# Order of weight loads, small stores and last steps in a one-core attention-and-MLP backward kernel

## Chip, core and metric

The kernel runs on one core of one Trainium2 chip. The metric is the device time of one execution in microseconds. Before the change three runs gave 430.39, 437.87 and 425.78 us, median 430.39.

## What is computed

The reference is one decode step of a gated mixture of a multi-head attention block over a K/V cache and a small MLP, and its gradients with respect to all inputs but the MLP's own x.

```python
x: [1, 1, 640]; k_cache, v_cache: [1, 32, 4096, 128]; wq: [640, 4096]; wo: [4096, 640]
w1: [640, 1728]; b1: [1728]; w2: [1728, 640]; gate_w: [640]; all bf16

g = sigmoid(sum(x * gate_w))
q = (x @ wq) as 32 heads of 128;  p = softmax(q . K * 128**-0.5);  a = (p . V) @ wo
h = B_x @ w1 + b1;  b = (h * tanh(softplus(h))) @ w2
out = g * a + (1 - g) * b
```

Outputs are `out` and the gradients of x, K, V, wq, wo, w1, b1, w2 and gate_w. dK and dV have the size of the caches: 67 MB are read for K and V and 67 MB written for their gradients. In the code out_2 is dK, out_3 dV, out_4 dwq, out_5 dwo, out_6 dw1, out_7 db1 and out_8 dw2.

## The kernel before

**Pairs and slots.** The 32 heads are worked through as 16 pairs (index i), each pair's K or V being one tile [128, 8192] of 2 MB. Eight such buffers (`kv0` to `kv7`) are in use. Every pair has 16 slots (function `slot`, line 687). In slots 0 to 7 TensorE transposes an eighth of V of pair i (line 342), ScalarE copies it out (`tch`, line 345), and two or three slots later products with the columns of dO make dP (line 352); slots 8 to 15 do the same with K of pair i+1 and q, for the scores S of the next pair. Between them lies the chain of the pair: maximum (slots 2 and 4), exponentials (5), sum (7), p (8), o (column sums on TensorE, 7 and 8, line 401), D (10), dS (11), and dq (13 and 14). dV is made over V in place by four VectorE outer products (slots 9, 10, 12, 13, line 433) and stored at slot 13; dK of pair i-1 is made over K (slots 15 of the pair before, 0, 1, 3) and stored at slot 3.

**Groups.** Four pairs form a group g of eight heads, with one slice of wq (`wqb`, [128, 5, 1024]) and one of wo (`wob`, [128, 8, 640]), both double-buffered by g % 2. Before a group starts, the kernel needs its query rows and columns (`q_half` twice, line 259, then `q_cols`, 268) and its dO rows and columns (`do_sum` eight times on VectorE, 271; `do_rows`, 275; `do_cols`, 283; `do_plain`, 286). After its pairs it makes the share of a (`o_rows`, 298; `a_cols`, 310), overwrites wo by dwo on ScalarE (`dwo_row`, eight times, 322) and stores it (`st_dwo`, 325), and for each of five row chunks takes dx's sum over wq on VectorE (`dx_sum`, 452) and overwrites wq by dwq on ScalarE (`dwq_row`, 457), then stores that (`st_dwq`, 460). Only then can the weights of group g+2 be loaded there (`ld_wo`, 152; `ld_wq`, 149).

**The order of the work** is written out by hand: `at(i, s, f, ...)` (line 593) hangs a step behind the body of slot s of pair i, and every engine runs its instructions in the order in which they are issued. `cols(i, s, g, c0, c1)` (line 596) hangs five `dx_sum` on slots s to s+4 and five `dwq_row` on s+1 to s+5, for the columns c0 to c1 of the group.

**Queues.** Loads are issued on SyncE (SP). `pump` (line 168) issues the next K or V load as soon as a buffer has been given back, right behind the step that stores it; on the chip SP then waits until that store has landed. Loads of weights wait in the same way for the store of the weights that they replace. Stores of dK, dV and the weights are issued on GpSimd (POOL) as long as loads are left, afterwards on SP. ScalarE (ACT) issues the db1 stores, the last part of dwo and the three final vectors.

**Scratch shared between steps.** All of `spread`, `q_half`, `pair_cols`, `do_rows`, `o_rows` and `a_cols` use one PSUM tile (`misc`), and `spread` and `pair_cols` share the SBUF tile `dup`.

**Start and end.** At the start SP issues the first loads, POOL the loads of x, gate_w, dy and b1 (lines 173 to 176) and then the identity `idf` (179 to 184). From x come the gate and, from it and dy, da and db; `spread` (234) broadcasts them over partitions. At the end (lines 795 to 843) pair 15 is written out without its slots 12 to 15: dV, dK in four quarters, dq, and the last share of a, wq, wo and the three vectors.

Of the kernel before, what the change touches and what calls it, by code (L numbers as in the profile page):

```python
# [17 lines left out]
def kernel(  # L18
# [83 lines left out]
    def C(shape, dt, name):  # L102
        return const.tile(shape, dt, name=name, tag=name)
# [64 lines left out]
    def pump():  # L168
        while loads and (free_q or not loads[0][0]):
            loads.popleft()[1]()  # L170

    pump()
    for t, src in ((xc[:], x_v), (gwc[:], vec_cols(gate_w)), (dyc[:], dy_v),
# [5 lines left out]
    idf = C([P, P], F32, "idf")  # L179
    nc.gpsimd.memset(idf[:], 0.0)  # L180
    nc.gpsimd.affine_select(
        out=idf[:], in_=idf[:], compare_op=ALU.not_equal, fill=1.0,
        base=0, pattern=[[-1, P]], channel_multiplier=1,
    )
# [382 lines left out]
    def mlp_dh():  # L567
        nc.vector.tensor_tensor(dh_b[:], dact[:], dm[:], ALU.mult)
        nc.scalar.dma_start(out_7[0:FM].rearrange("(p k) -> p k", k=FK), dh_b[:, 0:FK])
        nc.scalar.dma_start(out_7[FM:F].rearrange("(p o) -> p o", o=1), dh_b[0:FR, FK:FN])  # L570

    def mlp_dhrow(h):
        spread(dh_b[:, 0:FK], FK, 64 * h, 64 * h + 64, dh_bc[:, 64 * h * FK:(64 * h + 64) * FK])
        if h:
            ps = misc([P, FR], BF16, "dh_ps")
            nc.tensor.transpose(ps[:], dh_b[0:FR, FK:FN].to_broadcast([FR, P]), idb[0:FR, 0:FR])
            nc.scalar.copy(dh_bc[:, FM:F], ps[:])

# [14 lines left out]
    def at(i, s, f, *a):  # L593
        side.setdefault((i, s), []).append(lambda: f(*a))
# [6 lines left out]
    KC = 6 * Dh  # L601
    for g in range(1, NG):
        i = 4 * g - 1
        at(i, 4, q_half, g, 0)
        at(i, 6, q_half, g, 1)
        at(i, 8, q_cols, g)
        for k in range(8):
            if g == 1:
                at(i, (3, 4, 4, 5, 6, 7, 8, 8)[k], do_sum, g, k)
            else:  # L610
                at(i - 1, (3, 4, 5, 6, 7, 8, 14, 14)[k], do_sum, g, k)
        at(i, 10, do_rows, g)
        at(i, 12, do_cols, g)
        at(i, 14, do_plain, g)
    for g in range(NG):
        i = 4 * g + 3
        last = g == NG - 1
        at(i - last, 10, o_rows, g, 0, P - 32 * last)
        at(i - last, 11, a_cols, g)
        for k in range(8):  # L620
            at(i - last, 12 + k // 2, dwo_row, g, k, 0, P - 32 * last)
        if g == 0:
            cols(4, 4, 0, 0, GC)
        else:
            cols(i, 4, g, 0, KC)
            if not last:
                cols(i + 1, 4, g, KC, GC)
        if last:
            at(i, 0, st_dwo, g, nc.sync, 0, P - 32)
            at(i, 10, st_dwq, g, 0, KC, nc.sync)  # L630
        else:
            at(i + 1, 0, st_dwo, g, nc.gpsimd)
            at(i + 1, 10, st_dwq, g, 0, GC, nc.gpsimd)
            if g + 2 < NG:
                at(i + 1, 8, ld_wo, g + 2)
                at(i + 1, 15, ld_wq, g + 2)
# [134 lines left out]
    spread(da_c[:], RC, 0, P, da_bc[:])  # L771
    q_half(0, 0)
    q_half(0, 1)
    q_cols(0)
# [24 lines left out]
    for s in range(9, 12):  # L799
        slot(i, s)  # L800
    for t in (2, 3):
        outer(vbuf[i], st[i]["p"], Dr[g % 2][:, q, :], t)
    nc.sync.dma_start(dVv[i], bufs[vbuf[i]][:, 0:KVW])
    fb = free_q.popleft()
# [4 lines left out]
    col_sum(i, "dq", kbuf[i], ds_m[i % 2], 0, J)  # L809
    dq_row(i)  # L810
    o_rows(g, 32 * q, P)
    a_cols(g)
# [4 lines left out]
    for k in range(8):  # L817
        dwo_row(g, k, 32 * q, P)
    st_dwo(g, nc.scalar, 32 * q, P)
# [54 lines left out]
```

## Time and profile before

| | |
|---|---|
| median of three runs | 430.39 us (425.78 to 437.87) |
| profiled execution | 430.21 us, its span 428.4 us |
| mean granted TensorE clock | 0.872 |
| busy: TensorE matmul, VectorE, ScalarE | 315.7, 278.2, 269.2 us |
| DMA | 164.89 MB, mean 385 GB/s |
| SP's wait for dK and dV stores | 303.4 us in 26 waits |
| ScalarE's wait for transposes (line 342) | 58.5 us in 65 waits |

The span runs from the first to the last instruction of the profiled execution; the profile's DMA rows cut it in 40 slices of 10.71 us. A digit is the busy share in tenths, and 9 is 90% or more. The row of GB/s tells what the sixteen DMA engines moved. In a timeline row the bracket gives the engine's idle time ahead of the instruction and what ended it; POOL and SP rows ending in `DMA_DIRECT2D` are issues, not transfers. A row of a table of stretches has the stretch, its length, then for PE, PEld (weight load), DVE, ACT and POOL the busy time and the number of instructions, then the granted TensorE clock, the DMA engines' busy share and GB/s.

Pair i begins its first slot (by the `tch` copies of line 345) at these times: 34.3, 53.9, 74.6, 98.4, 137.0, 158.7, 183.3, 199.6, 241.4, 256.1, 273.6, 299.7, 335.3, 350.0, 365.7 and 390.1 us.

### The profile page before, as it was taken

How to read it: one execution, taken by the hardware profiler on the slowest of the kernel's cores; microseconds unless marked ns; L12 is line 12 of the kernel's file. 1: busy time of each engine (PE TensorE's matmuls, PEld its weight loads, DVE VectorE, ACT ScalarE, POOL GpSimd, SP SyncE). 2: the span in 40 equal slices, each digit the busy share in tenths (PEclk: the TensorE clock that was granted, in tenths of full speed). 3: DMA queues.
4: the chain of work that ended last, by engine and by line, in shares of the span. 5: the costliest groups of instructions: out<-in, count | busy, mean ns of one | idle time of the engine just before them, and what ended most of it. 6: DMA issues, size and time to landing. Idle time of an engine off the chain costs nothing. (4 is left out here: it accounts for less than half of the span.)

```text
span 428.4 us, 13140 instructions
## 1 busy us (share of the span) xinstructions
PE 315.7 (74%) x5679; PEld 287.2 (67%) x5682; DVE 278.2 (65%) x612; ACT 269.2 (63%) x542; POOL 22.3 (5%) x45
## 2 busy tenths in 40 slices
PE   3569798886685896788667898829669899889320
PEld 3159698884684786677456897829558799878320
DVE  3271659997635894999435686737754696577950
ACT  3245455579657887575463987525485987759452
POOL 3000000001000010000000010000000000000000
PEclk9998899998957987999875999978896999979755
DMA  8999999999999999999999999999999997999781
GB/s 271 438 424 414 417 417 372 379 405 359 182 430 429 426 418 393 425 429 419 430 427 431 420 419 408 424 422 425 424 434 404 410 362 258 384 427 369 317 324 31
DMA packets 17465, 164.89 MB, mean 385 GB/s; under 512 B 2288, under 2 KB 3632, under 8 KB 7680
## 3 DMA queue, kind: packets, MB, share of 16 engines
q1 hardware_dynamic: 11328, 101.09, 58.6%
q0 software_dynamic: 5376, 62.63, 36.3%
q8 instruction: 44, 0.72, 0.6%
q10 hardware_dynamic: 704, 0.34, 0.5%
q14 instruction: 13, 0.11, 0.1%
HBM read 82.03 MB, written 82.03 MB: 383 GB/s over the span
## 5 line engine op out<-in xcount | busy, mean ns | idle before, releaser
L345 ACT COPY tch<-tr 128x512 f32<-128x512 f32 x256 | 145.8, 587 | 64.8 <-PE tr L342 58.5
L342 PE MATMUL tr<-idf,kv 128*128 128x128 f32 x1024 | 177.1, 301 | 8.5 <-DMA kv<-in_A_k_cache_dram 8.5
L342 PEld LDWEIGHTS tr<-idf,kv 128*128 128x128 f32 x1024 | 122.7, 154 | 15.7 <-issue 13.7
L352 PEld LDWEIGHTS <-tch 128*128 128x128 bf16 x2048 | 91.7, 100 | 43.4 <-ACT tch L345 35.5
L433 DVE TENSOR_TENSOR kv<-ds_dup,Qr 128x2048 bf16<-128x2048 bf16 x64 | 76.6, 1220 | 2.9 <-ACT tch L345 1.5
L433 DVE TENSOR_TENSOR kv<-p_dup,Dr 128x2048 bf16<-128x2048 bf16 x64 | 76.9, 1219 | 0.7 <-ACT p_dup L392 0.3
L401 PEld LDWEIGHTS <-kv 128*128 128x128 bf16 x2048 | 63.5, 100 | 7.1 <-DVE ds_m L423 3.9
L352 PE MATMUL dP<-dR,tch 128*128 128x48 bf16 x1024 | 48.5, 187 | 21.5 <-ACT tch L345 21.1
L352 PE MATMUL S<-qR,tch 128*128 128x48 bf16 x1024 | 49.8, 189 | 9.3 <-ACT tch L345 6.6
L401 PE MATMUL dq<-ds_m,kv 128*128 128x48 bf16 x1024 | 34.6, 191 | 6.4 <-DVE ds_m L423 6.2
L401 PE MATMUL o<-e_m,kv 128*128 128x48 bf16 x1024 | 32.6, 186 | 0.0
L272 DVE SCALAR_TENSOR_TENSOR junk<-wo,da_bc 128x640 bf16<-128x640 bf16 x32 | 26.3, 821 | 8.2 <-DMA wo<-in_A_wo_dram 7.5
L323 ACT ACTIVATE wo<-da_bc,o8f 128x640 bf16<-128x640 bf16 (+2 forms) x40 | 30.6, 822 | 0.1
L458 ACT ACTIVATE wq<-dqrow,xf 128x768 bf16<-128x768 bf16 (+2 forms) x35 | 26.9, 781 | 3.5 <-DVE wq L454 3.0
L680 POOL DMA_DIRECT2D out_dram<-kv x24 | 12.9, 538 | 264.9 <-DVE kv L433 226.9
L454 DVE SCALAR_TENSOR_TENSOR wq<-wq,dqrow 128x768 bf16<-128x768 bf16 (+2 forms) x35 | 25.4, 761 | 0.2
L407 DVE TENSOR_TENSOR o<-o,rz 128x2 f32<-128x2 f32 x16 | 2.5, 158 | 31.4 <-PE o L401 31.4
L262 PE MATMUL q_ps<-wq,xc 128*128 128x512 bf16 x37 | 13.8, 505 | 8.4 <-DMA wq<-in_A_wq_dram 6.9
L379 ACT ACTIVATE e_m<-S,negM 64x64 bf16<-64x64 f32 x32 | 10.5, 328 | 12.4 <-DVE negM L374 11.9
L386 DVE RECIPROCAL rz<-z 128x2 f32<-128x2 f32 x16 | 2.7, 170 | 23.3 <-PE z L384 23.2
L392 ACT ACTIVATE p_dup<-e_m,rz 64x128 bf16<-64x128 bf16 x32 | 12.7, 397 | 5.5 <-DVE rz L386 4.9
L374 DVE TENSOR_REDUCE negM<-mt 64x1 f32<-64x64 f32 x32 | 7.1, 222 | 12.6 <-PE mt L371 11.8
(162 smaller groups left out, 252.7 us busy)
## 6 DMA issues: line engine op xcount, KB each, us to landing
out_dram<-kv POOLq DMA_DIRECT2D x24, 2048.0 KB, 17.2
kv<-in_A_v_cache_dram SPq DMA_DIRECT2D x16, 2048.0 KB, 19.4
kv<-in_A_k_cache_dram SPq DMA_DIRECT2D x15, 2048.0 KB, 18.8
out_dram<-kv SPq DMA_DIRECT2D x7, 2048.0 KB, 14.9
wq<-in_A_wq_dram SPq DMA_DIRECT2D x4, 1280.0 KB, 34.3
wo<-in_A_wo_dram SPq DMA_DIRECT2D x4, 1280.0 KB, 22.6
out_dram<-wo POOLq DMA_DIRECT2D x3, 1280.0 KB, 12.1
out_dram<-wq POOLq DMA_DIRECT2D x3, 1280.0 KB, 14.5
```

Of the source, the lines that this page charges most:

```text
L262: nc.tensor.matmul(ps[:].rearrange("p a h d -> p (a h d)"), lhsT=xc[:, rc:rc + 1].to_broadcast([P, P]), rhs=wqb[g % 2][:, rc, a * 512:(a + ...
L272: nc.vector.scalar_tensor_tensor(junk[:], in0=wob[g % 2][:, k, :], scalar=1.0, in1=da_bc[:], op0=ALU.mult, op1=ALU.mult, accum_out=do8[g % ...
L323: nc.scalar.mul(wob[g % 2][p0:p1, k, :], da_bc[p0:p1, :], o8f[p0:p1, k:k + 1])
L342: nc.tensor.transpose(tp[:, t, :], src[:, 4 * c + t, :], idf[:])
L345: nc.scalar.copy(dst[:].rearrange("p a b e -> p (a b e)").bitcast(F32), tp[:].rearrange("p a b -> p (a b)"))
L352: nc.tensor.matmul(ps[:, 4 * B:4 * B + W].rearrange("p (a b) -> p a b", b=4), lhsT=src[:, t, :, e], rhs=col[:, e, :, :].rearrange("p a b - ...
L392: nc.scalar.activation(p[HS[hh]], e_m[i % 2][HS[hh], :, hh].unsqueeze(2).to_broadcast([64, J, 2]), ACT.Copy, scale=st[i]["rz"][HS[hh], hh: ...
L401: nc.tensor.matmul(st[i][key][:].rearrange("p (a b) -> p a b", b=2), lhsT=src[:, j, :], rhs=rhs[:, j, :].unsqueeze(1).to_broadcast([P, W / ...
L433: nc.vector.tensor_tensor(kview(b)[:, j0:j0 + n, :].rearrange("p j (a b) -> p j a b", b=2), col[:, j0:j0 + n, :].unsqueeze(2).to_broadcast ...
L454: nc.vector.scalar_tensor_tensor(w, in0=w, scalar=1.0, in1=dqrow[g % 2][:, c0:c1], op0=ALU.mult, op1=ALU.mult, accum_out=dq_acc[:, rc, par ...
L458: nc.scalar.mul(wqb[g % 2][:, rc, c0:c1], dqrow[g % 2][:, c0:c1], xf[:, rc:rc + 1])
L680: eng.dma_start(dst, bufs[b][:, 0:J * Dh])
```

## The change

- The identity is built on POOL ahead of the five small loads.
- db1 was stored from `dh_b` by two DMAs (13 values per partition, and one value in each of 64 partitions). It is now stored as one row of 1728 values from `dh_bc`, which holds db1's values in every partition, behind the last copy into it.
- In the start, the two `q_half` of group 0 go ahead of da's `spread`.
- For groups 1 to 3, `q_half` moves from slots 4 and 6 to 6 and 8 and `q_cols` from 8 to 9; for groups 2 and 3, `do_sum` moves from the pair before (slots 3 to 8, and two at 14) to two at slot 14 of that pair and six at slots 3 to 8 of the group's last pair before it starts.
- `cols` of groups 1 and 2 is cut in two halves of 512 columns, the first one pair earlier (pair 4g+2, slots 4 on), the second at pair 4g+4 from slot 2 on; before it was 768 columns at pair 4g+3 and 256 at 4g+4 from slot 4 on. Group 0 and the last group keep theirs.
- `st_dwq` of group 1 and 2 moves from slot 10 to 8. `ld_wo` moves from slot 8 to slot 1, right behind `st_dwo` in slot 0, and `ld_wq` from 15 to 11 (group 0) or 9 (group 1).
- At the end, the dq sum, `o_rows` and `a_cols` go ahead of the last two dV outer products, and `dq_row`, the dwo rows and their store ahead of the dK outer products.

```diff
+    (idf: memset and affine_select moved here)
     pump()
     for t, src in ((xc[:], x_v), (gwc[:], vec_cols(gate_w)), (dyc[:], dy_v), ...
         nc.gpsimd.dma_start(t, src)
-    (idf stood here)
...
     def mlp_dh():
         nc.vector.tensor_tensor(dh_b[:], dact[:], dm[:], ALU.mult)
-        nc.scalar.dma_start(out_7[0:FM].rearrange("(p k) -> p k", k=FK), dh_b[:, 0:FK])
-        nc.scalar.dma_start(out_7[FM:F].rearrange("(p o) -> p o", o=1), dh_b[0:FR, FK:FN])
...
             nc.scalar.copy(dh_bc[:, FM:F], ps[:])
+            nc.scalar.dma_start(out_7.rearrange("(o f) -> o f", o=1), dh_bc[0:1, :])
...
     for g in range(1, NG):
         i = 4 * g - 1
-        at(i, 4, q_half, g, 0)
-        at(i, 6, q_half, g, 1)
-        at(i, 8, q_cols, g)
+        at(i, 6, q_half, g, 0)
+        at(i, 8, q_half, g, 1)
+        at(i, 9, q_cols, g)
         for k in range(8):
             if g == 1:
                 at(i, (3, 4, 4, 5, 6, 7, 8, 8)[k], do_sum, g, k)
+            elif k < 2:
+                at(i - 1, 14, do_sum, g, k)
             else:
-                at(i - 1, (3, 4, 5, 6, 7, 8, 14, 14)[k], do_sum, g, k)
+                at(i, 1 + k, do_sum, g, k)
...
-            cols(i, 4, g, 0, KC)
-            if not last:
-                cols(i + 1, 4, g, KC, GC)
+            cols(i - 1, 4, g, 0, GC // 2)
+            cols(i + 1, 2, g, GC // 2, GC)
-            at(i + 1, 10, st_dwq, g, 0, GC, nc.gpsimd)
+        at(i + 1, 10 if g == 0 else 8, st_dwq, g, 0, GC, nc.gpsimd)
             if g + 2 < NG:
-                at(i + 1, 8, ld_wo, g + 2)
-                at(i + 1, 15, ld_wq, g + 2)
+            at(i + 1, 1, ld_wo, g + 2)
+            at(i + 1, 11 if g == 0 else 9, ld_wq, g + 2)
...
-    spread(da_c[:], RC, 0, P, da_bc[:])
     q_half(0, 0)
     q_half(0, 1)
+    spread(da_c[:], RC, 0, P, da_bc[:])
     q_cols(0)
...
+    col_sum(i, "dq", kbuf[i], ds_m[i % 2], 0, J)
+    o_rows(g, 32 * q, P)
+    a_cols(g)
     for t in (2, 3):
         outer(vbuf[i], st[i]["p"], Dr[g % 2][:, q, :], t)
     nc.sync.dma_start(dVv[i], bufs[vbuf[i]][:, 0:KVW])
+    dq_row(i)
+    for k in range(8):
+        dwo_row(g, k, 32 * q, P)
+    st_dwo(g, nc.scalar, 32 * q, P)
     fb = free_q.popleft()
     for t in range(4):
         outer(fb, st[i]["ds"], Qr[g % 2][:, q, :], t)
         h = slice(t * KVW // 4, (t + 1) * KVW // 4)
         nc.sync.dma_start(dKv[i][:, h], bufs[fb][:, h])
-    col_sum(i, "dq", kbuf[i], ds_m[i % 2], 0, J)
-    dq_row(i)
-    o_rows(g, 32 * q, P)
-    a_cols(g)
     for rc in range(RC):
         dx_sum(g, g, KC, GC, rc)
         dwq_row(g, KC, GC, rc)
     st_dwq(g, KC, GC, nc.sync)
-    for k in range(8):
-        dwo_row(g, k, 32 * q, P)
-    st_dwo(g, nc.scalar, 32 * q, P)
```

More of the change, by code (lines that the diff above doesn't have):

```diff
@@ L170, in pump @@
             loads.popleft()[1]()
-    pump()
-    for t, src in ((xc[:], x_v), (gwc[:], vec_cols(gate_w)), (dyc[:], dy_v),
-                   (b1c[:, 0:FK], B_b1[0:FM].rearrange("(p k) -> p k", k=FK)),
-                   (b1c[0:FR, FK:FN], B_b1[FM:F].rearrange("(p o) -> p o", o=1))):
-        nc.gpsimd.dma_start(t, src)
     idf = C([P, P], F32, "idf")
@@ L184 @@
     )
+    pump()
+    for t, src in ((xc[:], x_v), (gwc[:], vec_cols(gate_w)), (dyc[:], dy_v),
+                   (b1c[:, 0:FK], B_b1[0:FM].rearrange("(p k) -> p k", k=FK)),
+                   (b1c[0:FR, FK:FN], B_b1[FM:F].rearrange("(p o) -> p o", o=1))):
+        nc.gpsimd.dma_start(t, src)
     ones_b = C([P, 1], BF16, "ones_b")
@@ L599, in cols @@
             at(i, s + 1 + rc, dwq_row, g, c0, c1, rc)
-    KC = 6 * Dh
     for g in range(1, NG):
         i = 4 * g - 1
-        at(i, 4, q_half, g, 0)
-        at(i, 6, q_half, g, 1)
-        at(i, 8, q_cols, g)
+        at(i, 6, q_half, g, 0)
+        at(i, 8, q_half, g, 1)
+        at(i, 9, q_cols, g)
         for k in range(8):
@@ L614 @@
         at(i, 14, do_plain, g)
-    for g in range(NG):
+    for g in range(NG - 1):
         i = 4 * g + 3
-        last = g == NG - 1
-        at(i - last, 10, o_rows, g, 0, P - 32 * last)
-        at(i - last, 11, a_cols, g)
+        at(i, 10, o_rows, g)
+        at(i, 11, a_cols, g)
         for k in range(8):
-            at(i - last, 12 + k // 2, dwo_row, g, k, 0, P - 32 * last)
+            at(i, 12 + k // 2, dwo_row, g, k)
+        at(i + 1, 0, st_dwo, g, nc.gpsimd)
         if g == 0:
@@ L624 @@
         else:
-            cols(i, 4, g, 0, KC)
-            if not last:
-                cols(i + 1, 4, g, KC, GC)
[L628 to L632, printed above, removed]
-            at(i + 1, 10, st_dwq, g, 0, GC, nc.gpsimd)
-            if g + 2 < NG:
-                at(i + 1, 8, ld_wo, g + 2)
-                at(i + 1, 15, ld_wq, g + 2)
+            cols(i - 1, 4, g, 0, GC // 2)
+            cols(i + 1, 2, g, GC // 2, GC)
+        at(i + 1, 10 if g == 0 else 8, st_dwq, g, 0, GC, nc.gpsimd)
+        if g + 2 < NG:
+            at(i + 1, 1, ld_wo, g + 2)
+            at(i + 1, 11 if g == 0 else 9, ld_wq, g + 2)
+    KC = 6 * Dh
+    g, i = NG - 1, NP - 1
+    at(i - 1, 10, o_rows, g, 0, P - 32)
+    at(i - 1, 11, a_cols, g)
+    for k in range(8):
+        at(i - 1, 12 + k // 2, dwo_row, g, k, 0, P - 32)
+    at(i, 0, st_dwo, g, nc.sync, 0, P - 32)
+    cols(i, 4, g, 0, KC)
+    at(i, 10, st_dwq, g, 0, KC, nc.sync)
     at(0, 12, lambda: spread(db_c[:], RC, 0, P, db_bc[:]))
@@ L803 @@
     nc.sync.dma_start(dVv[i], bufs[vbuf[i]][:, 0:KVW])
+    dq_row(i)
+    for k in range(8):
+        dwo_row(g, k, 32 * q, P)
+    st_dwo(g, nc.scalar, 32 * q, P)
     fb = free_q.popleft()
```

## Prediction

> **What bounds the kernel now.** I read the page first, for engines and DMA.
>
> ```profile
> span 428.4 us, 13140 instructions
> PE 315.7 (74%) x5679; PEld 287.2 (67%) x5682; DVE 278.2 (65%) x612; ACT 269.2 (63%) x542; POOL 22.3 (5%) x45
> ...
> DMA  8999999999999999999999999999999997999781
> GB/s 271 438 424 414 417 417 372 379 405 359 182 430 429 426 418 393 425 429 419 430 427 431 420 419 408 424 422 425 424 434 404 410 362 258 384 427 369 317 324 31
> DMA packets 17465, 164.89 MB, mean 385 GB/s; under 512 B 2288, under 2 KB 3632, under 8 KB 7680
> ```
>
> No engine is full, the DMA nearly is. At the 430 GB/s of its good slices, 164.89 MB take 383.5 us; the span is 45 us longer. Summing (1 - GB/s / 430) x 10.71 us over the slices puts about 21 us of that before 344 us (4.0 in the first slice, 6.2 in the eleventh) and 24 after. Second, the list of waits from 36 to 400 us: who waits for a load?
>
> ```profile
> DVE junk L272 <- DMA wo<-in_A_wo_dram: 7.5, 1, 7.5
> PE q_ps L262 <- DMA wq<-in_A_wq_dram: 6.9, 2, 4.2
> PE tr L342 <- DMA kv<-in_A_k_cache_dram: 2.6, 1, 2.6
> ```
>
> K and V are late once, weights three times, and the engines lose 17 us. Loads run well ahead: K of pair 15 lands at 342.75 + 14.5 = 357 and is transposed at 374, V at 358.06 + 10.6 = 369 against 390. So a chain of computation with four holes runs beside a DMA that has little left to give. The timeline gives the holes their places:
>
> ```profile
> 284.75 0.83 DVE L272 SCALAR_TENSOR_TENSOR junk<-wo,da_bc 128x640 bf16<-128x640 bf16 x1 [7.47 <-DMA wo<-in_A_wo_dram]
> ...
> 208.54 1.45 PE L262 MATMUL q_ps<-wq,xc 128*128 128x512 bf16 x4 [4.18 <-DMA wq<-in_A_wq_dram]
> ...
> 217.99 0.63 PE L342 MATMUL tr<-idf,kv 128*128 128x128 f32 x4 [2.56 <-DMA kv<-in_A_k_cache_dram]
> ...
> 307.17 1.24 PE L262 MATMUL q_ps<-wq,xc 128*128 128x512 bf16 x4 [2.76 <-DMA wq<-in_A_wq_dram]
> ```
>
> They lie in pairs 10, 7, 7 and 11. Behind the first, DVE holds the negated maximum of slot 4, so ACT's exponentials wait 7.83 us and PE 7.86. Third, two-microsecond stretches of the eleventh slice:
>
> ```profile
> 108.00:110.00 2.00, 2.00 (x36) 1.59 (x34) 0.25 (x2) 1.94 (x7) 0.00 (x0) 1.00 1.12 98
> 110.00:112.00 2.00, 2.00 (x66) 1.89 (x61) 0.65 (x2) 1.90 (x5) 0.00 (x0) 1.00 0.93 98
> 112.00:114.00 2.00, 1.06 (x15) 1.06 (x15) 1.88 (x7) 0.60 (x3) 0.00 (x0) 1.00 0.85 115
> 114.00:116.00 2.00, 1.10 (x23) 1.00 (x19) 2.00 (x5) 1.17 (x2) 0.00 (x0) 1.00 0.75 139
> ```
>
> Last columns: DMA share about 1, GB/s about 110: the engines are held, not idle. The second db1 store (2 bytes per partition) is issued at 95.47 and lands 21.2 us later, at 116.7, just where this ends.
>
> **The change part by part** (one profiled execution: 430.21 us, span 428.4, so 1.8 around it; the median of the three runs is 430.39).
>
> *db1.* It removes two ACT-queue issues (0.38 + 0.56 us) and 192 small packets at slot 14 of pair 2, and adds one issue of 3.4 KB behind the last ACT copy of slot 15 of pair 3, a wait on ACT's own work. In 107 to 117 us the DMA moved 167 GB/s, so it lost 6.1 us. If the 2-byte packets cause this, about 6 us come back to the DMA. On the chain it is 0 here: in pair 3 nothing waits for a load. Bounds 0 and -6. I take 0 on the chain and -6 on the DMA's limit, because a limit is all it touches.
> The Trainium skill (DMA: Bandwidth & Descriptors, section Specifications) says that transfers below 512 B cost a read-modify-write. By that alone the 26-byte packets of the first store should hurt too, and that rule prices no neighbour: by it the sum is the same. In the packet records the 16 KB store packets stay at 0.61 us while the 26-byte ones pass, and take 2 to 3.5 us once the 2-byte ones do.
>
> *idf ahead of the pump, query rows ahead of da.* On POOL the memset and select (0.26 + 0.29) go ahead of five issues, so x, gate_w and dy come 0.55 us later; idf comes 2.8 us earlier, and the first transpose waits for K (5.95), not idf. On PE the first q_half stood behind da's spread at 14.57; its weights land at 1.18 + 9.8 = 11.0. Now: q_half 11.0 to 13.3, Qr 0.74, second q_half to about 16.9, Qr 17.7, then spread (0.59, 0.59, 0.27, 0.27) to 19.8. DVE's query copy (L248), at 20.80 before, shares the tile dup with the spread and starts at about 19.5. Gain 1.3, bounds 0 and 3.6 (14.57 - 11.0); I take 1, since da, which do_sum needs, is later than before (14.5 to 19.8).
>
> *Weights of groups 2 and 3 earlier, used later.* SP waits for the weight store to land, then issues. wo of group 3: its store issues at 241.83 and lands in 10.0, so 251.8 instead of 261.92. wq: 251.07 + 14.5 = 265.6, less about 2 for the two slots that its store moves up, instead of 276.43. Group 2: 134.53 + 14.0 = 148.5 for 157.69, and 152.35 + 8.2 = 160.6 for 170.52. Ten microseconds each. Queued behind these waits on SP are K and V loads, but those wait for stores that went out later on the same POOL queue, so the wait itself holds nothing; what is new is that V of pair 7 and K of pair 12 move behind a wq load. On the consumer side six of eight do_sum go from pair g-1 to slots 3 to 8 of the next, q_half from slots 4, 6 to 6, 8. Both move more than any hole is long, so the holes go: 7.5 (wo), 4.2 and 2.8 (wq), 2.6 (K of pair 8, which sat behind wq: it landed 39.2 us after its issue). Another 1 for PE at half clock right after (dP products 0.50 instead of 0.36 us). Together -18.1. Bounds: 0 if other loads are as late, -18.1. I take -18.1: it is a sum of measured waits, and the next loads have 9 us or more in hand.
>
> *The query chain gets tighter.* Slot 8 now holds q_half and slot 9 q_cols, while the first score products read qR in slot 10. Counted from slot 8's start at full clock: transposes, dP, o (0.48, 0.20, 0.82), q_half 1.1, Qr 0.74, then DVE's dup copy behind a V outer product (1.22) at about 4.1, 0.43, PE 0.63, qR 0.74: score products at 6.1 us. Before, in pair 11, 313.90 to 318.06 = 4.2. So +1.9 for each of three groups, +5.7; bounds 0 (ACT and DVE slack absorb it) and +7.8 (2.6 each where two do_sum lie in slot 8 too). I take the worked value.
>
> *dx columns in halves.* DVE does as much, elsewhere: 5 x 0.73 of 512 columns in pairs 4g+2 and 4g+4 (estimated between the 0.95 and 0.42 us rows of 768 and 256) for 5 x 1.03 in 4g+3 and 5 x 0.44 in 4g+4. Pairs 6 and 10 lose six do_sum (5.4) and gain 3.65: -1 each after slack. Pairs 8 and 12 run at the floor of 14.7 us and gain 5 x (0.73 - 0.44) = 1.45: +1.4 each. Sum +0.8; bounds -3.6 and +2.9.
>
> *The tail.* From the last ds_m (401.65): o_rows and a_cols come first, behind the dq sum (2.74 at half clock): 404.4 + 0.3 + 0.9 + 1.77 gives a_acc at 407.6, so the last two V outer products end at 410.0, not 404.0, and V's store is 6 us later. Then dqb, four K outer products to 414.7, dx 1.7, the final vectors 2 to 2.5. ACT gets dqrow at 411.0, eight dwo rows 5.83 to 416.8, its store, five dwq rows to 418.9, then the three vector issues, the last ending at 420.8 instead of 422.94. Before, those landed 5.7 us after issue behind the dwo store:
>
> ```profile
> 414.81 5.83 ACT L323 ACTIVATE wo<-da_bc,o8f 32x640 bf16<-32x640 bf16 x8
> ...
> 420.67 0.34 ACTq L326 DMA_DIRECT2D out_dram<-wo  x1
> ...
> 422.54 0.40 ACTq L843 DMA_DIRECT2D out_dram<-fin  x1
> ```
>
> Now the dwo store is four microseconds ahead. K's quarters queue behind V: 410.3 + 4.9 + 4.9 = 420, plus dwq. Gain 3, bounds 5.5 and -1 (if V's store sets the end).
>
> Sum: -1 - 18.1 + 5.7 + 0.8 - 3 = -15.6, so 430.2 - 15.6 = 414.6, rounded to 415. The DMA's limit, as a check: 383.5, plus 21 - 6 before 344, plus about 12 for start of the last stores to landing = 410.5 span, 412 in time; the chain is the longer.
>
> **Rivals.** *The slow stretch stays.* Then the limit is 412 + 6 = 418 and the chain meets it. For it: 26-byte and 2-byte packets record 9 ns each, too little to fill eight microseconds. Against: no other stretch is like it.
> *The chain gives back half:* other loads are late (K of pair 12, needed at about 304 less what was gained), the query chain stalls at its upper bound: -18.1 becomes -9, +5.7 becomes +7.8: 426.
> *The wq load holds up K and V (slower).* In 184 to 196 us the two queues advance packet for packet, whatever their sizes:
>
> ```profile
> q0 software_dynamic: 289, 4.36, 85.6%
> q1 hardware_dynamic: 288, 0.69, 14.7%
> ```
>
> So 40 packets of 2 KB per engine take 40 x 0.67 = 27 us while the store queue has work; with it empty (294 to 298, 521 packets) a quarter of that. If it has work throughout, V of pair 7 lands at 168 + 27 + 10 = 205 (needed at 199.6) and K of pair 12 at 275 + 27 + 10 = 312 (slot 8 stood at 313.9). The -18.1 becomes 0: 432.5. It decides once the store queue stays full for all 27 us of both loads; against it, stores run at nearly the full rate meanwhile and so run out.
> The Trainium skill (DMA: Bandwidth & Descriptors, section Queues, rings and completion order) has engines turn between queues per packet, of 9 to 17 descriptors; the rows show single ones. By the page's figure a load needs only 3 to 5 turns, so this rival would cost less.
> *More comes back:* the DMA gap at 354 to 360 us (163 GB/s) closes too and the tail gains 5.5: 408.
>
> **How the numbers follow.** Forecast (412 to 421) 0.42, slow stretch stays 0.13, more comes back 0.08, half given back 0.20, held up 0.12, something the trace doesn't show 0.05. A measurement here tells about 2% (8.6 us): faster means under 421.8. Faster: 0.42 + 0.13 + 0.08 = 0.63. Slower (over 439): a third of "held up" and the unseen, 0.09. Same: 0.28. The range 406 to 428 leaves out "held up" and the unseen, 0.17; the forecast's own is 412 to 421.
>
> **What would show it.** Right: no DVE wait on wo and no PE wait on wq after 36 us; pair 10 near 18 us instead of 26; no slice under 350 GB/s near 110 us; the last ACT issue two microseconds nearer to ds_m. Wrong: PE waits on K or V near pairs 7 and 11, wq loads that still land 30 us after issue, score products waiting on qR by over 2 us in slot 10, or a V store that lands last.

## The result, and the profile after

The changed kernel takes 433.46 us (median of 20 runs, 430.56 to 438.33), the kernel before in the same session 429.48 us (median of 20). The ratio is 1.012 (95% interval 1.0083 to 1.0157): it is slower by 1.2%, about 5 us. The medians are of all executions and lie 4.0 us apart; this ratio and those below are of executions outside a second, slower state that both kernels show. The prediction was 415 us, with a range of 406 to 428.

The page of the changed kernel (its profiled execution took 431.76 us, of which the span is 430.0) has hardly moved as a whole:

```profile
span 430.0 us, 13140 instructions
PE 314.7 (73%) x5682; PEld 284.9 (66%) x5682; DVE 278.6 (65%) x612; ACT 268.0 (62%) x542; POOL 22.3 (5%) x45
...
DMA  8999999989999999999999999999998899958383
GB/s 282 434 431 404 425 410 417 428 322 413 429 393 391 368 400 424 399 420 434 419 434 421 425 422 432 425 421 431 433 424 364 325 362 396 420 232 332 146 339 112
```

The eleventh slice is at 429 GB/s instead of 182, and the last five give it back (they sum to 1161 instead of 1468). The list of waits from 36 to 400 us shows the trade. VectorE's 7.5 us for wo are gone, and TensorE's wait for wq is one long one:

```profile
PE q_ps L262 <- DMA wq<-in_A_wq_dram: 15.7, 1, 15.7
PE tr L342 <- DMA kv<-in_A_k_cache_dram: 3.6, 1, 3.6
```

The times at which pairs begin tell where. How far the changed kernel is ahead of the one before, in us:

| pair | 0 | 3 | 4 | 7 | 8 | 10 | 11 | 12 | 13 | 15 | last ds_m | end of span |
|---|---|---|---|---|---|---|---|---|---|---|---|---|
| lead | 5.1 | 2.6 | 0.6 | 1.9 | 12.1 | 11.7 | 20.4 | 1.8 | -0.3 | 0.1 | 0.0 | -1.6 |

Pair 7 is shorter by 10.2 us and pair 10 by 8.7, as foreseen. Pair 11 then takes 54.2 us instead of 35.6 and gives nearly all of it back. TensorE's timeline in that pair:

```profile
300.50 2.29 PE L262 MATMUL q_ps<-wq,xc 128*128 128x512 bf16 x5 [15.69 <-DMA wq<-in_A_wq_dram]
...
308.63 1.09 PE L342 MATMUL tr<-idf,kv 128*128 128x128 f32 x4 [3.61 <-DMA kv<-in_A_k_cache_dram]
...
315.92 0.36 PE L352 MATMUL S<-qR,tch 128*128 128x48 bf16 x8
```

TensorE reached `q_half` at 300.50 - 15.69 = 284.8, where before it came at 307.17 - 2.76 = 304.4: 19.6 us earlier. The weights came only 6.7 us earlier (300.5 instead of 307.2). The difference, 13 us, is the longer wait. K of pair 12 is 3.6 us late after that, and from there (308.63, slot 8) to the first score product are 7.3 us.

Why was wq of group 3 late? The DMA issues in 250 to 278 us of the kernel before and in 236 to 271 of the changed one (operation, KB, median us from issue to landing) show the store of dwq that must land first, then the load:

```profile
out_dram<-wq POOLq DMA_DIRECT2D x1, 1280.0 KB, 14.5
...
wq<-in_A_wq_dram SPq DMA_DIRECT2D x1, 1280.0 KB, 30.7
```

```profile
out_dram<-wq POOLq DMA_DIRECT2D x1, 1280.0 KB, 31.1
...
wq<-in_A_wq_dram SPq DMA_DIRECT2D x1, 1280.0 KB, 31.4
```

The store was issued 13.2 us earlier (237.90 for 251.07) and took 16.6 us longer to land, at 269.05, so the request came at 269.1 (before: 276.4). In the kernel before it was not dwq's store (landed at 265.5) that held the request: a K load stood ahead of it on SP (issued at 275.98), which had waited for a dK or dV store that landed at 275.8. The load's 640 packets (40 on each engine, 2 KB each) then passed between 272.9 and 299.5 us, 26.6 us; before, between 292.4 and 306.0, 13.6 us. Who else had packets in these stretches (q0 the store queue, q1 the loads; packets, MB, share)? First the kernel before, then the changed one:

```profile
q1 hardware_dynamic: 841, 4.00, 71.3%
q0 software_dynamic: 122, 1.72, 30.1%
```

```profile
q0 software_dynamic: 624, 9.00, 79.8%
q1 hardware_dynamic: 706, 2.21, 20.6%
```

Before, the stores had 122 packets in the way of 841; now 624 against 706, nearly one for one, and 79.8% of the DMA's time went to them. The reason stands in POOL's timeline, in the issues of dK and dV stores. Before:

```profile
277.57 0.53 POOL L680 DMA_DIRECT2D out_dram<-kv  x1 [6.33 <-DVE kv L433]
298.61 0.53 POOL L680 DMA_DIRECT2D out_dram<-kv  x1 [20.50 <-DVE kv L433]
```

and after:

```profile
277.71 0.53 POOL L683 DMA_DIRECT2D out_dram<-kv  x1 [11.05 <-DVE kv L433]
284.54 0.53 POOL L683 DMA_DIRECT2D out_dram<-kv  x1 [6.30 <-DVE kv L433]
```

While VectorE stood still for wo in pair 10, no outer product was finished and no store issued for 21 us; the store queue ran empty, and wq came through. Without that wait the gap at this place is 11 us. Two stores of 2 MB are issued in the stretch in which wq is loading, and what is still queued from the stores before makes up the rest of the 9.00 MB.

The end, in the timeline of the changed kernel (two issues on ACT's queue) and in its DMA issues from 416 us on:

```profile
416.58 0.34 ACTq L326 DMA_DIRECT2D out_dram<-wo  x1
...
419.59 1.99 ACTq L846 DMA_DIRECT2D out_dram<-fin  x1
```

```profile
out_dram<-wo ACTq DMA_DIRECT2D x1, 320.0 KB, 10.1
...
out_dram<-fin ACTq DMA_DIRECT2D x3, 1.2 KB, 9.7
```

The dwo store goes out 4.1 us earlier than before and lands in 10.1 us instead of 6.0: in the packet records its packets run only from 420 to 422 us, behind the K quarters that are queued on the other queue. The last issue ends at 421.58, 1.4 us earlier than before, but the vectors land after 9.7 us instead of 5.7. V's store landed at 416.1; what landed last are these small stores and that of dwq (428.9), whose packets also follow K's. From the start of the last ds_m to the end of the span are 29.0 us (before 27.4).

### The profile page after: what moved, and what is told of

The parts are those of the page before. It is cut to its first block, busy times and chain, and to the rows that moved or that the text cites. A ratio compares the mean times of both kernels' runs of the same rounds, so it can differ in the third digit from the quotient of the medians.

```text
span 430.0 us, 13140 instructions
## 1 busy us (share of the span) xinstructions
PE 314.7 (73%) x5682; PEld 284.9 (66%) x5682; DVE 278.6 (65%) x612; ACT 268.0 (62%) x542; POOL 22.3 (5%) x45
## 4 chain that ended last, share of the span: by engine, by line
issue 51%; DMA 19%; PE 11%; ACT 7%; DVE 5%; POOL 3%; SPq 1%; POOLq 0%; ACTq 0%
DMA kv<-in_A_k_cache_dram 8%; DMA out_dram<-kv 7%; DMA kv<-in_A_v_cache_dram 4%; PE tr L342 4%; DVE kv L433 3%; ACT tch L345 3%; PE dq L401 2%; POOL out_dram L683 2%; PE a_ps L315 1%; ACT wq L458 1%; PE o L401 1%; PE S L352 1%; ACT wo L323 1%; ACT e_m L379 1%; PE dP L352 1%
## 5 line engine op out<-in xcount | busy, mean ns | idle before, releaser
L342 PE MATMUL tr<-idf,kv 128*128 128x128 f32 x1024 | 178.1, 303 | 10.1 <-DMA kv<-in_A_k_cache_dram 9.7
L342 PEld LDWEIGHTS tr<-idf,kv 128*128 128x128 f32 x1024 | 123.5, 155 | 17.7 <-issue 15.9
L352 PEld LDWEIGHTS <-tch 128*128 128x128 bf16 x2048 | 90.5, 100 | 40.3 <-ACT tch L345 33.7
L352 PE MATMUL dP<-dR,tch 128*128 128x48 bf16 x1024 | 48.2, 186 | 14.4 <-ACT tch L345 13.9
L458 ACT ACTIVATE wq<-dqrow,xf 128x512 bf16<-128x512 bf16 (+3 forms) x35 | 27.0, 785 | 0.7 <-DVE amb L834 0.4
L454 DVE SCALAR_TENSOR_TENSOR wq<-wq,dqrow 128x512 bf16<-128x512 bf16 (+3 forms) x35 | 25.5, 763 | 1.9 <-ACT dqrow L450 1.7
L407 DVE TENSOR_TENSOR o<-o,rz 128x2 f32<-128x2 f32 x16 | 2.5, 159 | 35.2 <-PE o L401 35.1
L262 PE MATMUL q_ps<-wq,xc 128*128 128x512 bf16 x40 | 12.6, 457 | 17.0 <-DMA wq<-in_A_wq_dram 16.1
L266 ACT CAST Qr<-q_ps 64x256 bf16<-64x256 f32 x16 | 5.9, 367 | 24.1 <-PE q_ps L262 24.1
L262 PEld LDWEIGHTS <-xc 128*128 128x128 bf16 x40 | 4.2, 115 | 21.7 <-issue 19.4
## 6 DMA issues: line engine op xcount, KB each, us to landing
out_dram<-kv SPq DMA_DIRECT2D x7, 2048.0 KB, 11.8
```

The source lines that it names most:

```text
L262: nc.tensor.matmul(ps[:].rearrange("p a h d -> p (a h d)"), lhsT=xc[:, rc:rc + 1].to_broadcast([P, P]), rhs=wqb[g % 2][:, rc, a * 512:(a + ...
L342: nc.tensor.transpose(tp[:, t, :], src[:, 4 * c + t, :], idf[:])
L352: nc.tensor.matmul(ps[:, 4 * B:4 * B + W].rearrange("p (a b) -> p a b", b=4), lhsT=src[:, t, :, e], rhs=col[:, e, :, :].rearrange("p a b - ...
L454: nc.vector.scalar_tensor_tensor(w, in0=w, scalar=1.0, in1=dqrow[g % 2][:, c0:c1], op0=ALU.mult, op1=ALU.mult, accum_out=dq_acc[:, rc, par ...
L458: nc.scalar.mul(wqb[g % 2][:, rc, c0:c1], dqrow[g % 2][:, c0:c1], xf[:, rc:rc + 1])
```

## The experiments

The theory: each packet of the wq load waits for one 16 KB store packet as long as stores are queued, and the wait for wo had kept that queue empty. The rivals: the earlier requests take DMA time from K and V; the later uses make the chain longer; the new end alone is the loss. A ratio of 0.01 is 4.3 us.

**The four parts alone.**

```diff
 before + db1 stored as one row                            (e1)
 before + idf ahead of the loads, q_half ahead of spread   (e2)
 before + weight requests, do_sum, q_half, q_cols, cols    (e3)
 before + new end                                          (e4)
```

> The kernel before with only the db1 store changed to one row. Theory A (the 2-byte packets cause the slow stretch, and the DMA's backlog decides when group 3's wq lands): no stretch near 110 us under 350 GB/s, wq of group 3 lands about 6 us earlier than at 307, total 3 to 6 us less. Theory B (the stretch has another cause, or the chain doesn't feel it): the stretch stays or goes, the total moves by less than 2 us.

Measured: 427.18 us, ratio 0.9933 (0.9874 to 0.9992), about 2.9 us faster. From 106 to 116 us the DMA now moves 418 to 442 GB/s in each two microseconds, so the two old db1 stores made the slow stretch. That it is the one of 2 bytes rests on the packet times in the prediction; this edit takes out both. The chain gains in pair 7: wq of group 2 lands at 202.4 instead of 208.5, TensorE no longer waits for it, and pair 8 begins 4.8 us earlier. VectorE's wait for wo in pair 10 grew to 12.6 us, and pair 11 begins only 0.4 us earlier, but wq of group 3 lands 5.3 us earlier, and pair 12 begins 4.5 us earlier.

> The kernel before with only the start changed (identity first, query rows ahead of da's spread). Theory A (a lead of the computation is given back at the next late weight load): pair 0 begins 5 us earlier, at 29, and the lead is gone by pair 11; total within 2 us of before. Theory B (the terms of the chain add up): total 5 us less.

Measured: 428.17 us, 0.9933 (0.9897 to 0.9969), about 2.9 us faster. Pair 0 begins at 32.7, 1.6 us earlier and not 5, and pair 11 begins 1.9 us later than before: the lead is gone by then, as Theory A has it, but the total gains more than its 2 us. The waits for weights stay: wq 12.5 us (11.8 of them for group 2), wo 7.0.

> The kernel before with only the weight requests, the do_sum, q_half, q_cols and dx columns moved. Theory A (the wq load of group 3 lands when the DMA's backlog lets it, whatever the chain does): pairs 7 and 10 are shorter by about 10 and 8 us, TensorE then waits over 10 us for wq in pair 11 and for K behind it; total 2 to 6 us more. Theory B (the schedule gains, the tail and db1 lose): 10 us less.

Measured: 438.0 us, 1.0179 (1.0149 to 1.0209), 7.7 us slower. The part that was to bring 18 us is the one that loses. Its wq packets of group 3 pass in 280.6 to 306.8 us, TensorE waits 15.5 us for them and 3.8 for K, and pair 12 begins at 340.9 instead of 335.3.

> The kernel before with only the end changed. Theory A (V's last store, 6 us later, sets the end through the stores queued behind it): 1 to 3 us more. Theory B (the prediction's tail: the dwo store no longer sets the end): 3 us less.

Measured: 433.4 us (429.14 to 436.3, four runs, too far apart for a ratio). In its profile the end takes 29.1 us from the last ds_m, against 27.4 before, and the vectors land after 9.7 us. That is the changed kernel's end, without the rest of the change. The time alone doesn't tell them apart.

**Is it wq of group 3?** (e5: the changed kernel leaves out this load, and group 3's query rows, dx and dwq are made from the old contents of the buffer)

```diff
-            at(i + 1, 11 if g == 0 else 9, ld_wq, g + 2)
+            if g == 0:
+                at(i + 1, 11, ld_wq, g + 2)
```

> The changed kernel without the load of group 3's wq (1.3 MB; group 3's query rows, dx and dwq are computed from what lies in the buffer). Theory A (the changed kernel waits in pair 11 for this load, and K of pair 12 stands behind it): pair 11 no longer stalls, pair 12 begins 15 us or more earlier than the changed kernel's 333, total 13 to 18 us less than the changed kernel, about 417. Theory B (the DMA's total amount of data sets the end): 3 us less, the share of 1.3 MB.

Measured: 418.1 us, 0.9769 (0.9715 to 0.9823), some 15 us below the changed kernel. Pair 11 takes 32.1 us, and after 36 us TensorE waits 0.3 us for K, VectorE and ScalarE for no load. The 1.3 MB that are not moved make up 3 us at 430 GB/s. The whole loss, and some 10 of the 15.6 us that were foreseen, hang on this one load.

**Is it the size of the packets?** All transfers of K, V, dK and dV in quarters (4 KB per partition): in the changed kernel (e6), in the kernel before with the first two parts (e8), and, of the edit, the stores' lines only in the changed kernel (e10). e7 is the kernel before with the first two parts and no quarters.

```diff
-        eng.dma_start(dst, bufs[b][:, 0:J * Dh])
+        for t in range(4):
+            h = slice(t * KVW // 4, (t + 1) * KVW // 4)
+            eng.dma_start(dst[:, h], bufs[b][:, h])
...
-        loads.append(ld_kv(kbuf, i, Kv[i], 1))
+        loads.append(ld_kv(kbuf, i, Kv[i], 4))
```

> The changed kernel with every K, V, dK and dV transfer cut into four, so that their packets are 4 KB instead of 16 KB and a wq load's 2 KB packets take turns with shorter ones. Theory A (the alternation of packets makes wq late): wq of group 3 lands within 15 us of its issue instead of 31, TensorE's wait in pair 11 falls below 6 us, total 8 us or more less than the changed kernel, about 424. Theory C (wq is late because everything queued ahead of it has to move first): landing and total within 3 us of the changed kernel.

Measured: 421.41 us, 0.9841 (0.9782 to 0.99), 12 us below the changed kernel. TensorE waits 3.8 us for wq. Its packets pass in 18.3 us (270.6 to 288.9); the request came 7.7 us earlier (261.4), and the load still landed only 28.2 us after it (31.4 in the changed kernel). So of the 10.9 us by which wq is read earlier, 7.7 are the earlier request. While wq passes, 1182 load packets stand against 1180 store packets: K's and V's, now small too, lie between wq's 640 in the same queue, and each takes its turn.

> The kernel before with the db1 row and the new start alone. Theory A (both shorten what stands ahead of the wait for group 3's weights, one on the DMA's side and one on the chain's): gains of 2.9 us each add up, about 425. Theory B (they fill the same wait): no more than either alone, 427 to 428.

Measured: 430.59 us, but four runs between 422.1 and 434.83, which is no measurement of a few microseconds. Inconclusive.

> The kernel before with the db1 row, the new start and the transfers of 4 KB packets. Theory A: the waits for wo and wq in pairs 7, 10 and 11 shrink by half or more, total 5 to 12 us less than with db1 row and start alone, 413 to 420. Theory C (the amount of data queued ahead is what counts): within 3 us of them.

Measured: 423.46 us, 0.9897 (0.981 to 0.9984). Without the new order the wait for wo stays (6.4 us), the wait for wq is gone.

> The changed kernel with only the dK and dV stores cut into four; loads keep 16 KB packets. Theory A (wq's packets wait for one store packet each): group 3's wq needs about 40 x 0.24 = 10 us from its first packet to its last instead of 27, and the total comes near that with all transfers cut, 420 to 424. Theory D (it is the load packets that hold up the stores of dwq, and so the request): no nearer than half way, 427 or more.

Measured (the changed kernel with only the stores in quarters): 424.9 us, 0.9875 (0.9815 to 0.9936). Between 274.9 and 285.8 us, when wq of group 3 passes:

```profile
q0 software_dynamic: 701, 2.56, 58.3%
q1 hardware_dynamic: 699, 1.82, 42.5%
```

Again packet against packet, 701 to 699, but a store packet is now a quarter, and the 40 turns take 10.9 us instead of 26.6. No wait for wq is left. This shows the mechanism: it is the store packets that the load waits for, one each.

**The old end, and the old places of the query rows, with small packets.**

The old end undoes the last part of the change, in e6's kernel (e9) and in the changed kernel (e13):

```diff
-    col_sum(i, "dq", kbuf[i], ds_m[i % 2], 0, J)
-    o_rows(g, 32 * q, P)
-    a_cols(g)
     for t in (2, 3):
         outer(vbuf[i], st[i]["p"], Dr[g % 2][:, q, :], t)
...
-    dq_row(i)
-    for k in range(8):
-        dwo_row(g, k, 32 * q, P)
-    st_dwo(g, nc.scalar, 32 * q, P)
     fb = free_q.popleft()
...
+    col_sum(i, "dq", kbuf[i], ds_m[i % 2], 0, J)
+    dq_row(i)
+    o_rows(g, 32 * q, P)
+    a_cols(g)
...
+    for k in range(8):
+        dwo_row(g, k, 32 * q, P)
+    st_dwo(g, nc.scalar, 32 * q, P)
```

> The changed kernel with 4 KB packets and the end of the kernel before. Theory A (the new end holds V's last store back by 6 us and costs 1 to 2 us): 1 to 3 us less than the changed kernel with 4 KB packets, 419. Theory B (the prediction's tail): 3 us more, 424.

Measured: 420.73 us, 0.9793 (0.9748 to 0.9837), against 421.41 and 0.9841 of the same with the new end: 0.7 us by the medians, 2 by the ratios. The intervals overlap, and by themselves these two leave the end open.

In e9's kernel, the query rows go back to their old slots (e11):

```diff
-        at(i, 6, q_half, g, 0)
-        at(i, 8, q_half, g, 1)
-        at(i, 9, q_cols, g)
+        at(i, 4, q_half, g, 0)
+        at(i, 6, q_half, g, 1)
+        at(i, 8, q_cols, g)
```

> As the one with 4 KB packets and the old end, but q_half and q_cols in slots 4, 6 and 8 as before the change. Theory A (the tighter query chain costs 2 to 3 us in each of three groups, and wq is in time now but in group 3): 2 to 6 us less, 413 to 417. Theory B (wq's landing sets pair 11 in either place): the same within 2 us.

Measured: 419.52 us (418.77 to 419.91), 0.9768 (0.9732 to 0.9803). Within 2 us of the run before it, and 14 us below the changed kernel.

> The changed kernel with the end of the kernel before. Theory A (the new end costs 1 to 3 us through V's later store): 1 to 3 us less than the changed kernel, 430.5 to 432.5. Theory B (the prediction's tail gains 3): 436 or more.

Measured (the changed kernel with the old end): 432.19 us, 1.0039 (0.9995 to 1.0084), where the new end gives 1.012. In its profile the end takes 27.7 us from the last ds_m instead of 29.0. So the new end costs 1.3 us by the profiles, and 3.5 by the ratios, whose intervals just overlap. In the eight other profiles with 16 KB stores and the old end it takes 27.4 to 28.2 us, with the new end 29.0 and 29.1 (the changed kernel and e4).

**The new order, taken apart.**

```diff
-                at(i + 1, 8, ld_wo, g + 2)      (e12 and e15)
+                at(i + 1, 1, ld_wo, g + 2)
-                at(i + 1, 15, ld_wq, g + 2)     (e12 alone)
+                at(i + 1, 11, ld_wq, g + 2)
```

e14 is the reverse of e12, the new order without these two lines:

```diff
 e3
-            at(i + 1, 1, ld_wo, g + 2)
-            at(i + 1, 11 if g == 0 else 9, ld_wq, g + 2)
+            at(i + 1, 8, ld_wo, g + 2)
+            at(i + 1, 15, ld_wq, g + 2)
```

> The kernel before with only the weight requests moved up (wo to slot 1, wq to slot 11), uses as before. Theory A (earlier requests help where the queue lets the data through; what wo gains, wq's wait takes): VectorE no longer waits for wo, TensorE waits for wq in pair 11 longer than 2.8 us, total within 4 us of before. Theory E (the requests alone do the harm, by putting wq ahead of K and V): 4 us or more above before.

Measured: 435.21 us, 1.0108 (1.0035 to 1.0181). VectorE's wait for wo is gone, TensorE waits 18.6 us for wq, whose packets pass in 26.1 us with 612 store packets among them.

> The kernel before with only the uses moved (do_sum, q_half, q_cols, dx columns, dwq's store two slots earlier), the weights requested in slots 8 and 15 as before. Theory A (of the schedule's loss the requests alone make 4.6, the tighter query chain the rest): 2 to 4 us above before; TensorE waits for wq in pair 11 all the same, because the chain gets there earlier than the load. Theory F (only early requests hurt; later uses give the loads time): 3 us or more below before.

Measured (uses moved, requests left in slots 8 and 15): 444.32 us, 1.0326 (1.0261 to 1.0391), 14 us slower. No number above foresaw that. TensorE waits 20.0 us for wq of group 3 and 6.7 for K in pair 7. The request goes out at 276.7, as before the change, and wq is read at 314.7, 7.5 us later than before; pair 12 begins 7.9 us later and the last pair 10.9. The mechanism is the same one: VectorE's wait for wo in pair 10 is gone here too, since the sums that read wo come a pair later, and wq passes among 342 store packets in 20.5 us (before: 122 in 13.6). These 6.9 us are most of the 7.5; the rest of the 14 is not traced.

> The kernel before with only wo's request moved up, to slot 1; wq stays at 15. Theory A (wq, not wo, is what meets a full store queue, but it also is what the chain then waits for): VectorE's wait for wo in pair 10 goes, TensorE's wait in pair 11 takes its place; total within 3 us of before. Theory G (any request moved up hurts): 4 us or more above before, as with both.

Measured: 441.12 us, 1.0249 (1.0194 to 1.0303), 10.7 us slower. It was expected within 3 us, so the theory lacked something. The timeline of its pair 11:

```profile
311.75 0.59 PE L262 MATMUL q_ps<-wq,xc 128*128 128x512 bf16 x1 [23.82 <-DMA wq<-in_A_wq_dram]
```

Moving a request of 1.3 MB by seven slots took the wait for wo away, shortened pair 7 too (31.7 us for 41.8), and made wq come 4.6 us later than in the kernel before. What was lacking is the other half: with the chain running on, the store queue stays full. The store of dwq lands after 29.1 us instead of 14.5, at 272.5; the request stands on SP behind a K load that waits for a dK or dV store until 278.0 (before: 275.8) and goes out 2.6 us later. Its packets then begin 0.9 us earlier than before (291.5), but meet 352 store packets (122 before) and pass in 19.6 us instead of 13.6. Behind the start of pair 12 another 4 us are lost, 2.5 of them in pair 12 itself; the cause of these is open.

**Three more, on what that left open.** Small store packets with and without the request of wo moved, and small packets with only the requests moved and all uses in their old places.

```diff
 e15 + stores in quarters                                      (e16)
 before + stores in quarters                                   (e17)
 e12 + db1 row + start + loads and stores in quarters          (e18)
```

> The kernel before with wo's request moved from slot 8 to slot 1, as in the run where that alone cost 10.7 us, and now the dK and dV stores cut in quarters (4 KB packets). Theory A (the wait for wo had kept the store queue empty while wq of group 3 was loading; without it each 2 KB load packet takes turns with a 16 KB store packet): with 4 KB store packets a turn costs about 0.17 + 0.1 us instead of 0.67, so wq's 40 packets of group 3 pass in 10 to 14 us instead of 19.6, TensorE waits for wq in pair 11 under 8 us instead of 23.8, and the time is at least 12 us below that run's: about 420 to 429, that is 0 to 10 us under the kernel before. Theory B (the early request of wo does harm by taking DMA time from K and V, whatever the store packets): still 5 us or more above the kernel before.

> The kernel before with the dK and dV stores in quarters and nothing else. Theory A: VectorE's wait for wo in pair 10 (7.5 us) stays within 2 us, since wo is requested as late; wq of group 3 already found the store queue empty (13.6 us) and gains little; 0 to 5 us under the kernel before, and not more than 4 us under the run that has wo's request moved too. Theory B (small store packets are worth as much alone as with the early requests, so the changed kernel's loss has nothing to do with the stores' packets): 8 us or more under the kernel before, and wo's wait in pair 10 gone.

Measured: 428.89 us, 0.9998 (0.9953 to 1.0043), and 428.73 us, 0.9993 (0.9945 to 1.0042). So the 10.7 us are gone with small store packets, and wq passes in 10.7 us, as Theory A had it. It was wrong on both waits: TensorE's for wq is 14.5 us where under 8 was expected, and VectorE's for wo, without the request moved, 14.8 where it should have stayed at 7.5. The timelines of the first and of the second:

```profile
303.71 0.59 PE L262 MATMUL q_ps<-wq,xc 128*128 128x512 bf16 x1 [14.55 <-DMA wq<-in_A_wq_dram]
```

```profile
284.49 0.83 DVE L272 SCALAR_TENSOR_TENSOR junk<-wo,da_bc 128x640 bf16<-128x640 bf16 x1 [14.78 <-DMA wo<-in_A_wo_dram]
...
304.82 1.24 PE L262 MATMUL q_ps<-wq,xc 128*128 128x512 bf16 x4 [0.44 <-DMA wq<-in_A_wq_dram]
```

These two are the clearest runs of the study. The second waits 14.8 us for wo in pair 10, the first not at all there but 14.5 for wq in pair 11; wq is requested at 284.5 us in the second and 283.9 in the first and read at 304.8 and 303.7, pair 12 begins at 331.7 and 332.0, and the time is the same. A wait ahead of a later, fixed arrival cost nothing by itself here, and taking it away gained nothing.

> The kernel before with db1 as one row, the new start, only the requests for wo and wq moved up (slots 1 and 11), the old places of do_sum, q_half, q_cols and dx columns, the old end, and all K, V, dK and dV transfers in quarters. Theory A (with small packets the early request is what helps, and the later uses do nothing or cost): within 3 us of the best run so far (419.5 us), with no weight wait over 4 us after 36 us. Theory B (the moved uses are needed): 4 us or more above it, with a VectorE or TensorE wait for weights of 4 us or more in pairs 7, 10 or 11.

Measured: 419.93 us (419.87 to 420.68), 0.9798 (0.9739 to 0.9857), within half a microsecond of the best run. TensorE's wait for wq is 0.2 us, VectorE's for wo 1.8, and V costs TensorE 2.2. With small packets the early requests suffice; the moved uses, the halves of dx and the new end are not needed. Without the early requests the same kernel is e8, at 0.9897: about 4 us by the ratios, whose intervals overlap, so small packets with the db1 row and the new start have part of the gain already. This one and the run with 419.52 us are the two fastest kernels.

What orders these kernels up to pair 12, in all the traces, is when TensorE reads wq of group 3 (us from the start of the span):

| kernel | dwq stored | wq requested | packets pass | wq read | pair 12 begins | span |
|---|---|---|---|---|---|---|
| before | 251.1 | 276.4 | 13.6 | 307.2 | 335.3 | 428.4 |
| changed | 237.9 | 269.1 | 26.6 | 300.5 | 333.5 | 430.0 |
| e3, new order alone | 245.3 | 276.8 | 26.2 | 308.0 | 340.9 | 436.1 |
| e14, uses alone | 249.5 | 276.7 | 20.5 | 314.7 | 343.2 | 439.6 |
| e15, wo's request alone | 243.4 | 279.1 | 19.6 | 311.8 | 341.1 | 438.2 |
| e16, that and 4 KB stores | 246.1 | 283.9 | 10.7 | 303.7 | 332.0 | 427.6 |
| e10, changed, 4 KB stores | 241.6 | 268.5 | 10.9 | 288.3 | 316.2 | 422.7 |
| e18, requests, all 4 KB | 240.5 | 261.0 | 17.4 | 287.3 | 314.2 | 418.1 |
| e11, all 4 KB | 238.7 | 261.2 | 16.3 | 286.2 | 312.9 | 418.0 |

Pair 12 begins 27 to 29 us after wq is read, and 33 in the changed kernel and e3, where K of pair 12 is late as well (3.6 and 3.8 us). With the early request, the time from dwq's store to the request is 31.2 us in the changed kernel, 26.9 with stores in 4 KB packets (e10), and 22.5 and 20.4 with the loads in 4 KB packets too (e11, e18). That fits the same turns, taken by the dwq store's packets against 16 KB load packets; no run isolates it.

The lead at pair 12 doesn't all reach the end. In e18 the last ds_m starts 16.8 us earlier than in the kernel before, and the span is 10.3 us shorter: from there to the end are 33.9 us instead of 27.4 (36.7 in e11, 39.1 in e10), while the stores still queued are written. The DMA rows of e18:

```profile
DMA  8999999999999999999999999999999999999990
GB/s 262 429 430 402 403 414 417 417 416 415 426 412 417 421 344 403 412 395 423 413 417 417 421 412 420 414 412 417 417 418 417 419 415 378 402 393 353 370 377 17
```

## Why the prediction was wrong

**The step that failed** is "Weights of groups 2 and 3 earlier, used later", and in it "I take -18.1: it is a sum of measured waits, and the next loads have 9 us or more in hand". For group 2 it held: its wq packets passed in 167.6 to 177.1 us, and pair 7 is 10.2 us shorter. For group 3 it failed three times over. The request was worked out at 265.6 less 2 us from a landing of 14.5 us for the dwq store, and came at 269.1, since that store took 31.1. The load took 31.4 us, not less than before (30.7). And the place of use came 19.6 us earlier, with all the gains before it, so "in hand" was counted against a chain that does not speed up. A sum of waits is a gain only if whatever comes next does not arrive at a fixed time; here wq did. The equal times of e16 and e17 show it.

**The rival that came** is "The wq load holds up K and V", given 12% and 432.5 us; the measured 433.46 lies beside it. That the number is so close is in part luck: the rival has nothing gained in pairs 7 and 10 and nothing lost in pair 11, where 18.9 us were gained and 18.6 lost, and it keeps the tail's -3, which came out at +1.6. Its mechanism was right, 40 turns of 0.67 us = 27 us (measured 26.6), but for group 3 alone, and what it held up was wq itself (15.7 us) more than K (3.6). My argument against it, that stores "run at nearly the full rate meanwhile and so run out", failed because the wait that I removed was what let them run out.

The Trainium skill (DMA: Bandwidth & Descriptors, section Queues, rings and completion order) has an engine drain a packet of typically some 9 to 17 descriptors of one queue before it turns. The prediction took the rows with 289 beside 288 for turns of one, and concluded that by the page's figure the load would pass sooner. Equal counts alone don't say that: turns of nine against nine give them too, and the same time. The packet records do: put in line engine by engine, each record starting where another ends, 519 of 522 turns of the store queue between 274 and 299 us of the changed kernel are one packet long, and 457 of 531 of the load queue. The measurement decides.

**db1.** Right about the cause: the slow stretch is gone here and in e1. "0 on the chain" was too little for e1's 2.9 us: nothing waited for a load in pair 3, but wq of group 2 came 6.1 us earlier to a place that did wait. In the changed kernel that can't be told from the rest.

**The start.** -1 predicted, with a bound of 3.6; in these two profiles pair 0 begins 5.1 us earlier. The edit is not all of that: the `q_half` products of group 0 took 0.38 us each in this execution and 0.59 to 0.63 in the kernel before, and also in e2, which has the same start and gains 1.6; why is open. Over all profiles pair 0 begins at 32.4 us in the mean with the new start (eleven) and at 35.2 with the old (nine), 2.8 apart and inside the bound. Of the 5.1 us, 4.5 are lost again by pair 4: 2.0 in pair 3 and 2.2 in pair 2, where the granted clock differs: pair 2 takes 26.0 us at a granted clock of 0.87 in this and five other kernels, old and new, and 23.2 to 23.9 at 1.00 in the others.

**The query chain.** "+1.9 for each": pair 3 is 2.0 us longer (1.8 in the mean of all profiles, twelve with the old chain and eight with the new). Pair 11's slot 8 takes 7.3 us to the score products instead of 4.2: +3.1, beyond the bound of 2.6, but at a granted clock of 0.50 from 308 to 314 us, after the long wait. Right in pair 3, in pair 11 not to be told from the clock. With small packets, undoing it is worth under 2 us (e11 against e9).

**dx in halves.** +1.4 was given to pairs 8 and 12; they are 1.2 and 2.1 us longer. For pair 8 that holds in every profile: 14.6 to 14.8 us with the old columns, 15.9 to 16.0 with the new. Pair 12 doesn't show it: 14.7 to 17.2 with the old, 15.9 to 17.4 with the new.

**The tail.** "Gain 3" has the wrong sign: 1.6 us lost. The last issue did end earlier (421.58 instead of 422.94; 420.8 was worked out, which is 2.1 and not 3), but a landing no longer than the 5.7 us of before was taken for granted, and it became 9.7 behind the stores that the new order puts in front. The bound "-1 (if V's store sets the end)" is nearer as a number only: V's store landed 13.9 us before the end.

**The limit by the DMA**, 410 to 412 us, did not bind in the changed kernel. It is near in the fastest ones (419.5 and 419.9 us), whose end is longer by the stores still queued.

## What to carry to other kernels

Before adding up the waits of a profile, ask of each what arrives next and whether that arrival moves: a wait that ends before a later transfer lands is free, and removing it only moves the waiting. A stall on one engine can be what empties a queue for somebody else; when you remove it, redo the landing times with that queue full. Where a load in small packets runs beside stores in large ones, the number of packets in its queue, its own and those between, times the time of a store packet and its own is about its duration, so cut the large ones before asking earlier: here the early requests alone lost 4.6 us (e12), small store packets alone gained nothing (e17), and with small packets the early requests are in the fastest kernels (e11, e18).

## What the runs showed of the hardware

- The store queue of POOL and the load queue of SP take turns packet by packet, whatever the sizes: 640 packets of 2 KB on 16 engines passed in 26.6 us beside 16 KB store packets, in 10.9 beside 4 KB ones, at nearly the same total rate (425 and 405 GB/s in these stretches). At the end of the changed kernel ACT's queue got no such turns from SP's: the dwo store, issued at 416.58, moved its first packet at 420.6, when K's last were passing (before: 0.8 us after the issue). Why is open.
- Stores of very small packets slow others: without the two db1 stores (26 and 2 bytes per packet) the stretches from 108 to 114 us run above 400 GB/s, where the kernel before moved 98 to 115. The 16 KB store packets slowed once those of 2 bytes passed (from 105.3 us on); no run takes out one of the two stores alone. The changed kernel's stretches:

```profile
108.00:110.00 2.00, 2.00 (x55) 1.75 (x52) 0.56 (x5) 1.33 (x3) 0.00 (x0) 1.00 1.01 428
110.00:112.00 2.00, 1.39 (x16) 0.96 (x14) 1.97 (x7) 1.17 (x3) 0.00 (x0) 1.00 1.07 459
112.00:114.00 2.00, 0.64 (x6) 0.67 (x7) 1.22 (x2) 0.14 (x1) 0.00 (x0) 1.00 0.97 404
```

- A small store behind a backlog on another queue is slow at both ends: the three issues of the vectors took 1.03, 1.21 and 1.99 us (before 0.38, 0.86 and 0.40), and they landed after 9.7 us (before 5.7); with the new end alone (e4) 1.04, 1.20 and 2.06, and 9.7.
